# A hand-written order of pieces for VectorE, ScalarE and GpSimd in the attention part, from its ninth f-tile step

## The chip, the cores and the metric

The kernel runs on one core of one Trainium2 chip. The metric is the device time of one execution in microseconds (us); lower is better. The engines are TensorE (PE; its weight loads stand apart as PEld), VectorE (DVE), ScalarE (ACT), GpSimd (POOL) and SyncE (SP), which issues all of this kernel's data transfers (DMAs).

## The reference

Windowed attention with global tokens, a SiLU-gated two-matrix layer, and a second layer with a rational activation, on 4 batches of 544 rows (2176 rows of 512 values) in float32:

```python
def _attn_ref(q_l, k_l, v_l, q_g, k_g, v_g):
    ...
    s_g = scale * np.matmul(q_g, k_all.transpose(0, 1, 3, 2))
    out_g = np.matmul(sm(s_g), v_all)
    ...
    mask = np.abs(pos[:, None] - pos[None, :]) <= window
    s_ll = np.where(mask, s_ll, -1000000000.0)
    a_l = sm(np.concatenate([s_lg, s_ll], axis=-1))
    out_l = np.matmul(a_l, np.concatenate([v_g, v_l], axis=2))
    return np.concatenate([out_g, out_l], axis=2)

def _moe_ref(x, w_gate, w_val, w_out):
    g = x @ w_gate
    silu = g * (1.0 / (1.0 + np.exp(-g)))
    return (silu * (x @ w_val)) @ w_out

def _moe2_ref(x, w_in, w_out, a, b):
    h = x @ w_in
    P = a[0] + a[1] * h + a[2] * h * h + a[3] * h ** 3
    Q = 1.0 + np.abs(b[0]) * np.abs(h) + np.abs(b[1]) * h * h
    return (P / (Q + 1e-06)) @ w_out
```

The weights of the two layers arrive as float64. They are handed over as 64-bit words and made into float32 on the chip.

## The kernel before, in words

Three stages overlap: attention, the gated layer and the rational layer. A float32 product is made of three products of rounded halves (`mm3`, lines 526 to 528), so every operand of a layer is split into a high and a low half: ScalarE casts (L123, L374), VectorE subtracts (L126, L641).

Attention is cut into 24 units: a local unit is 128 rows of one batch, a global unit the 32 global rows of one batch, half of the heads. A unit passes through scores (`a_score`), the largest score (`a_least`, VectorE, L306 or L312 to L314), the exponentials (`a_exp`, ScalarE, L325 or L331 and L333), transposes (`a_turn`, L354), sums (`a_sums`, VectorE), copies to SBUF (`a_copy`, ScalarE), values (`a_value`), division (`a_norm`, VectorE, L427 or L433), a transpose back (`a_back`, L448) and a store into the rows x32 (`a_store`, VectorE, L374 or L461).

The gated layer's first four f-tiles of 128 (part "a") run while attention still goes on: 32 steps n = (row chunk c, f-tile). Steps 0 to 7, with the first nine units, are an order of words written by hand (`opening`). Steps 8 to 31 are a loop, four to a chunk of 256 rows (c = 2 and 4) or 288 rows (c = 3, 5, 6, 7). In a step TensorE makes the gate (12 matmuls), the transposes of unit t-1, the value product (12), the scores of unit t, the outward product of the step before (12, into four PSUM banks with the tag "a"), the values of unit t-1 and the transposes back of unit t-2. Steps 12, 20 and 27 to 31 have no attention. All other PSUM tiles have the tag "b" and share four banks in turn, so each waits for the readers of the tile four before it: the scores wait for the readers of the gate, the gate for those of the scores before, and so on.

Beside this the loop brings in the raw weights of the other f-tiles, 24 pieces: a DMA from HBM into a stage tile (`fetch`), a scaling on GpSimd (L141), a rounding on ScalarE (L143), two joins on VectorE (L144 and L146), and a DMA to the scratch w1s. When a chunk's four f-tiles are summed, `evac_a` copies the four banks (ScalarE L806, VectorE L804) into y tiles (four of them), and a DMA stores each to the scratch yas. In chunk 7 the weights come back from w1s and are split (ScalarE two casts, VectorE one subtraction, GpSimd one).

In the loop before, TensorE's and SP's order is the program's own. The order of VectorE, ScalarE and GpSimd is that of a planner, which has costs of its own for each operation and may move it ahead of others. From the gated layer's second part on (f-tiles 4 to 11, part "b") the order of all engines is the program's, in both kernels.

Of the kernel before, what the change touches and what calls it, by code (L numbers as in the profile page):

```python
# [21 lines left out]
S = SL + SG  # L22
# [55 lines left out]
def tile_attn_moe_moe(  # L78
# [48 lines left out]

    def fetch(src, pool, bufs):
# [7 lines left out]
    def to_f32(fetched):  # L136
        st, wide = fetched
        if wide:
            v = st.rearrange("p (c t) -> p c t", t=2)
            low, high = v[:, :, 0], v[:, :, 1]  # L140
            nc.gpsimd.tensor_scalar(out=high.bitcast(F32), in0=high.bitcast(F32), scalar1=2.0 ** -112,  # L141
                                    scalar2=1.0, op0=ALU.mult, op1=ALU.mult)
            nc.scalar.activation(low, low.bitcast(U32), AF.Copy, bias=0.25, scale=0.905 * 2.0 ** -29)  # L143
# [3 lines left out]
                                           op0=ALU.bitwise_and, op1=ALU.bitwise_or)  # L147
        return st[:, 0:512].bitcast(F32)
# [187 lines left out]
    def a_soft(u):  # L336
        for p in units[u][2] if units[u][1] < 4 else (0,):
            a_least(u, p)
            a_exp(u, p)

# [42 lines left out]

    def a_trans(u):
        ps_ = units[u][2] if units[u][1] < 4 else (0,)
        for p in ps_:
            a_turn(u, p)
        a_sums(u)
        for p in ps_:
            a_copy(u, p, nc.scalar)  # L390
# [45 lines left out]
    def a_pv(u):  # L436
        for p in units[u][2] if units[u][1] < 4 else (0,):
            a_value(u, p)
        a_norm(u)
        if u in local and local.index(u) + 2 < len(local):  # L440
            load_v(local[local.index(u) + 2])

# [21 lines left out]
    def a_out(u):  # L464
        a_back(u)
        a_store(u, nc.vector)

# [13 lines left out]
    def a_scores(u):  # L481
        a_loads(u)
        a_score(u)
        a_score2(u)
        a_soft(u)

    begun = set()

    def chunk_split(c, ks=range(4)):
        for k in ks:  # L490
            split_xy(("a", c), chunks_a[c], k)
# [4 lines left out]
    def attend(n, part):  # L496
        if n in step_at:
            t = step_at[n]
            for fn, u in (((a_trans, t - 1),), ((a_scores, t),), ((a_pv, t - 1), (a_out, t - 2)))[part]:
                if U0 <= u < NU or u == U0 - 1 and fn is not a_scores:  # L500
                    begun.add((fn, u))
                    fn(u)
# [46 lines left out]
    def hidden(key, f, w, inject):  # L549
        g = mlp(key, 0, f, w)  # L550
        s = p1.tile([128, N1P], F32, tag="s", name="s")
        h = p1.tile([128, 2, N1P], F32R, tag="h", name="h")
        if inject:
            nc.scalar.activation(s[:, :w], g[:, :w], AF.Tanh, scale=0.5)
            nc.vector.scalar_tensor_tensor(out=s[:, :w], in0=s[:, :w], scalar=1.0, in1=g[:, :w],
                                           op0=ALU.add, op1=ALU.mult)
            inject()
        else:
            nc.scalar.activation(s[:, :w], g[:, :w], AF.Silu)
        v = mlp(key, 1, f, w)  # L560
        if inject:
            nc.vector.scalar_tensor_tensor(out=s[:, :w], in0=s[:, :w], scalar=0.5, in1=v[:, :w],
                                           op0=ALU.mult, op1=ALU.mult)
        else:
            nc.vector.tensor_tensor(out=s[:, :w], in0=s[:, :w], in1=v[:, :w], op=ALU.mult)  # L565
        split(h[:, 0, :w], h[:, 1, :w], s[:, :w], nc.scalar, nc.vector)
        hs[key, f] = h
        if inject:
            inject()
# [92 lines left out]
    def w_scale(i):  # L662
        high = raw[i].rearrange("p (c t) -> p c t", t=2)[:, :, 1]
        nc.gpsimd.tensor_scalar(out=high.bitcast(F32), in0=high.bitcast(F32), scalar1=2.0 ** -112,
                                scalar2=1.0, op0=ALU.mult, op1=ALU.mult)

    def w_round(i, eng):
        lo = raw[i].rearrange("p (c t) -> p c t", t=2)[:, :, 0]
        nc.scalar.activation(lo, lo.bitcast(U32), AF.Copy, bias=0.25, scale=0.905 * 2.0 ** -29)

    def w_join(i):
        v = raw[i].rearrange("p (c t) -> p c t", t=2)
        lo, high = v[:, :, 0], v[:, :, 1]
        nc.vector.scalar_tensor_tensor(out=lo, in0=high, scalar=3, in1=lo,
                                       op0=ALU.logical_shift_left, op1=ALU.bitwise_or)
        nc.vector.scalar_tensor_tensor(out=raw[i][:, 0:512], in0=high, scalar=-2 ** 31, in1=lo,
                                       op0=ALU.bitwise_and, op1=ALU.bitwise_or)

# [8 lines left out]
    def act(word):  # L687
# [3 lines left out]
        u, p = (n + [0, 0])[:2]  # L691
# [35 lines left out]
        elif name in "FADHL":  # L727
            i = int(a)
            {"F": lambda: w_scale(i), "A": lambda: w_round(i, s), "D": lambda: w_join(i),
# [43 lines left out]
    state = {"n": 0}  # L773

    late = []

    def inject_a():
        g, i = state["g"], state["i"]
        c = seq_a[g][0]
        state["i"] = i + 1  # L780
        if c < NCA - 1:
            if i == 0 or i == 1 and g % 5 == 0:
                bg.end()
                bg.begin()
            else:
# [12 lines left out]

    def evac_a(c, j):
        for o, cols in [(0, chunks_a[0]), (HALF, chunks_a[1])] if c == 1 else [(0, chunks_a[c])]:  # L800
# [6 lines left out]
            for d, cc in xcols(cols):  # L807
                nc.sync.dma_start(yas[:, j, cc], y[:, d])
# [42 lines left out]
    for g, (c, f) in list(enumerate(seq_a))[2 * NA:]:  # L851
        if g == 8:
            loads["cb"]()
            loads["ca"]()
        if g == 16:
# [3 lines left out]
        state.update({"g": g, "i": 0})  # L859
        if (c, f) == (NCA - 1, 0):  # L860
            assert len(begun) == 4 * (NU - U0) + 3
# [5 lines left out]
            while bg.busy():  # L867
                bg.begin()
                bg.end()
            rest.prefetch(4)  # L870
        hidden(("a", c), f, w, inject_a)
# [286 lines left out]
```

## Time and profile before

| what | value |
|---|---|
| median of three runs | 938.31 us (934.78, 939.10, 938.31) |
| the profiled execution | 935.89 us |
| its span, first to last instruction | 934.1 us |
| TensorE busy in the span | 908.7 us (97%) |
| VectorE, ScalarE, GpSimd busy | 664.0, 569.4, 116.9 us |
| steps 8 to 31, by the start of their matmuls | 87.65 to 264.26 us of the span |

The profiled execution's own time is 1.8 us more than its span and lies between the three runs. Matmuls are pipelined, and the end of one is modelled: a matmul of 256 columns is shown with 0.28 us though the next starts 0.12 us after it.

### The profile page before, as it was taken

The page shows a single profiled execution, that of the slowest core. Times are in us where ns is not written, and L with a number is a line of the kernel's source. Part 1 is how long each engine was busy: PE and PEld are TensorE (multiplying, and loading weights), DVE is VectorE, ACT ScalarE, POOL GpSimd, SP SyncE. Part 2 cuts the span into 40 slices and gives each one's busy share as a digit, 9 for nine tenths or more (in the row PEclk, how much of TensorE's full clock was granted, in tenths as well). Part 3 has the DMA queues.
Part 4 walks back from the last instruction along what each step waited for, and adds up shares of the span by engine and source line. Part 5 has one row for each costly group of instructions (what it writes and reads, how often), then busy time and mean ns, then how long its engine had stood idle before and what let it go on. Part 6 is the DMA issues. An engine that isn't in the chain of part 4 may idle for free.

```text
span 934.1 us, 20234 instructions
## 1 busy us (share of the span) xinstructions
PE 908.7 (97%) x7893; PEld 845.8 (91%) x7895; DVE 664.0 (71%) x1578; ACT 569.4 (61%) x1348; POOL 116.9 (13%) x133
## 2 busy tenths in 40 slices
PE   6999999999999999999999999999999999999997
PEld 4789889788999999999999999999999999999896
DVE  4885778667735466555532569988889888888886
ACT  6764756555434344333322368888778788788796
POOL 1342010010303233111100001000000000000032
PEclk9999999999999999999999999999999999999999
DMA  9944996862551234454512230000010010010010
GB/s 330 370 148 156 318 345 219 285 233 83 167 197 46 89 98 140 147 183 153 177 57 72 77 105 1 1 22 13 1 35 0 1 35 1 1 35 1 1 35 24
DMA packets 51935, 102.76 MB, mean 110 GB/s; under 512 B 6912, under 2 KB 27008, under 8 KB 51840
## 3 DMA queue, kind: packets, MB, share of 16 engines
q1 hardware_dynamic: 51840, 101.47, 32.5%
q8 instruction: 62, 1.02, 0.4%
q14 instruction: 33, 0.27, 0.1%
HBM read 81.01 MB, written 20.45 MB: 109 GB/s over the span
## 4 chain that ended last, share of the span: by engine, by line
PE 84%; DMA 6%; DVE 4%; ACT 2%; issue 2%; SPq 1%; POOL 0%; POOLq 0%; ACTq 0%; DVEq 0%
PE b L526 15%; PE b L528 15%; PE b L527 15%; PE a L1056 7%; PE a L1055 6%; PE a L1054 6%; PE a L526 5%; PE a L527 4%; PE a L528 4%; DMA stage<-in_w_dram 4%; PE b L259 1%; PE b L354 1%; PE b L404 1%; DMA q<-in_qT_dram 1%; PE a L354 1%
## 5 line engine op out<-in xcount | busy, mean ns | idle before, releaser
L526 PE MATMUL b<-xy,wb 128*128 128x312 f32 (+3 forms) x632 | 197.5, 313 | 0.0
L528 PE MATMUL b<-xy,wb 128*128 128x312 f32 (+3 forms) x632 | 197.4, 312 | 0.0
L527 PE MATMUL b<-xy,wb 128*128 128x312 f32 (+3 forms) x632 | 197.4, 312 | 0.0
L526 PE MATMUL b<-xy,wa 128*128 128x256 f32 (+2 forms) x400 | 125.2, 313 | 5.8 <-DVE s L633 2.5
L527 PEld LDWEIGHTS b<-xy,wb 128*128 128x128 f32 x632 | 118.9, 188 | 2.5
L526 PEld LDWEIGHTS b<-xy,wb 128*128 128x128 f32 x632 | 118.9, 188 | 2.5
L527 PE MATMUL b<-xy,wa 128*128 128x256 f32 (+2 forms) x400 | 121.0, 302 | 0.0
L528 PE MATMUL b<-xy,wa 128*128 128x256 f32 (+2 forms) x400 | 120.9, 302 | 0.0
L528 PEld LDWEIGHTS b<-xy,wb 128*128 128x128 f32 x632 | 118.8, 188 | 0.0
L123 ACT CAST h<-s 128x312 fp32r<-128x312 f32 (+3 forms) x80 | 35.5, 444 | 118.2 <-DVE s L565 91.7
L565 DVE TENSOR_TENSOR s<-s,b 128x312 f32<-128x312 f32 (+1 forms) x56 | 26.7, 476 | 95.5 <-PE b L528 90.7
L1004 ACT ACTIVATE t<-b,cst 128x384 f32<-128x384 f32 (+1 forms) x94 | 61.3, 652 | 53.8 <-PE b L528 51.0
L526 PEld LDWEIGHTS b<-xy,wa 128*128 128x128 f32 x400 | 76.1, 190 | 9.3 <-DVE s L633 3.0
L1018 DVE TENSOR_TENSOR t<-t,b 128x384 f32<-128x384 f32 (+1 forms) x94 | 49.9, 531 | 41.5 <-ACT a L1005 41.3
L527 PEld LDWEIGHTS b<-xy,wa 128*128 128x128 f32 x400 | 75.8, 190 | 1.3
L528 PEld LDWEIGHTS b<-xy,wa 128*128 128x128 f32 x400 | 75.7, 189 | 0.0
L141 POOL TENSOR_SCALAR stage<-stage 128x512 f32<-128x512 f32 x56 | 39.2, 700 | 226.0 <-DMA stage<-in_w_dram 174.9
L1056 PE MATMUL a<-wb,g 128*128 128x512 f32 x170 | 67.1, 395 | 0.3 <-POOL g L1028 0.3
L1006 ACT ACTIVATE q<-a,cst 128x384 f32<-128x384 f32 (+1 forms) x94 | 64.9, 691 | 3.0
L1054 PE MATMUL a<-wb,g 128*128 128x512 f32 x170 | 66.3, 390 | 0.5 <-ACT g L1041 0.5
L1055 PE MATMUL a<-wb,g 128*128 128x512 f32 x170 | 66.7, 392 | 0.0
L126 DVE TENSOR_TENSOR h<-s,h 128x312 fp32r<-128x312 f32 (+3 forms) x80 | 39.4, 493 | 35.0 <-ACT h L123 34.8
(180 smaller groups left out, 2238.1 us busy)
## 6 DMA issues: line engine op xcount, KB each, us to landing
stage<-in_w_dram SPq DMA_DIRECT2D x68, 512.0 KB, 4.3
v<-in_vw_dram SPq DMA_DIRECT2D x16, 512.0 KB, 6.6
v<-in_vw_dram SPq DMA_DIRECT2D x16, 384.0 KB, 5.1
w1s<-stage SPq DMA_DIRECT2D x24, 256.0 KB, 5.3
stage<-w1s SPq DMA_DIRECT2D x12, 512.0 KB, 5.5
w2s<-stage SPq DMA_DIRECT2D x20, 256.0 KB, 2.4
stage<-w2s SPq DMA_DIRECT2D x10, 512.0 KB, 4.0
out_dram<-x SPq DMA_DIRECT2D x17, 256.0 KB, 2.8
```

The costliest lines, as they stand in the source:

```text
L123: nc.scalar.copy(hi, src)
L126: eng_lo.tensor_tensor(out=lo, in0=src, in1=hi.bitcast(F32), op=ALU.subtract)
L141: nc.gpsimd.tensor_scalar(out=high.bitcast(F32), in0=high.bitcast(F32), scalar1=2.0 ** -112, scalar2=1.0, op0=ALU.mult, op1=ALU.mult)
L526: nc.tensor.matmul(o, w[:, 0, wsl], x[:, 0, xsl], start=first, stop=False)
L527: nc.tensor.matmul(o, w[:, 0, wsl], x[:, 1, xsl], start=False, stop=False)
L528: nc.tensor.matmul(o, w[:, 1, wsl], x[:, 0, xsl], start=False, stop=last)
L1004: nc.scalar.activation(pt[n], h, AF.Identity, bias=NA2, scale=NA3)
L1006: nc.scalar.activation(pq[n], a, AF.Identity, bias=B0, scale=B1)
L1018: nc.vector.tensor_tensor(out=t, in0=t, in1=h, op=ALU.mult)
L1054: nc.tensor.matmul(o, g[:, 0, gsl], w[:, 0], start=(f == 0), stop=False)
L1055: nc.tensor.matmul(o, g[:, 0, gsl], w[:, 1], start=False, stop=False)
L1056: nc.tensor.matmul(o, g[:, 1, gsl], w[:, 0], start=False, stop=(f == F2 - 1))
```

## The change

Two things change in steps 8 to 31. First, VectorE, ScalarE and GpSimd follow a written list, as TensorE and SP do. A step is a line of words, one line for steps whose unit t is local, one for the rest, and one for chunk 7. A word is a piece: G gate, V value, O outward, t tanh, g and v the two multiplications, h and l the halves of the hidden tile, T R C P N S M E X Z the pieces of attention in the order of the list above (R sums, C copies, P values, N division, S scores, M largest, E exponentials, X back, Z store), F A D W the raw weight's scaling, rounding, joins and store, y and Y the halves of the next chunk's rows, e the copies of finished sums, w their stores, r a weight of chunk 7, q the loads of later units. The order of TensorE's own pieces is as before.

Second, work is moved between steps. A raw weight is scaled in one step, and rounded, joined and stored in the next; five steps (11, 16, 22, 24, 25) scale two, so that steps 12, 17, 23, 25 and 26 round and join two. The stores of finished sums are put off to a later word, mostly in the next step. The rows of chunks 4 and 5 are split in steps 14 and 15, and 18 and 19. The loads of queries, keys and values of later units are issued at a step's end, and look one unit further ahead.

The diff, cut to its core (helpers that only changed their name or were no longer called are left out):

```diff
...
-    def hidden(key, f, w, inject):
+    def hidden(key, f, w):
         g = mlp(key, 0, f, w)
         s = p1.tile([128, N1P], F32, tag="s", name="s")
         h = p1.tile([128, 2, N1P], F32R, tag="h", name="h")
-        if inject:
-            nc.scalar.activation(s[:, :w], g[:, :w], AF.Tanh, scale=0.5)
-            nc.vector.scalar_tensor_tensor(out=s[:, :w], in0=s[:, :w], scalar=1.0, in1=g[:, :w],
-                                           op0=ALU.add, op1=ALU.mult)
-            inject()
-        else:
-            nc.scalar.activation(s[:, :w], g[:, :w], AF.Silu)
+        nc.scalar.activation(s[:, :w], g[:, :w], AF.Silu)
...
-    def inject_a():
-        g, i = state["g"], state["i"]
-        c = seq_a[g][0]
-        state["i"] = i + 1
-        if c < NCA - 1:
-            if i == 0 or i == 1 and g % 5 == 0:
-                bg.end()
-                bg.begin()
-            else:
-                bg.end()
-        if c < NCA - 1:
-            attend(g, i)
-            if seq_a[g + 1][0] > c and i:
-                chunk_split(c + 1, (2 * i - 2, 2 * i - 1))
-        for _ in range(2):
-            if late and late[0][0] < state["n"]:
-                late.pop(0)[1]()
-        state["n"] += 1
-        if c == NCA - 1 and (3 * g + i) % 2:
-            rest.begin()
-            rest.end()
+    stores = []
+    def put_stores():
+        while stores:
+            stores.pop(0)()
...
-                nc.sync.dma_start(yas[:, j, cc], y[:, d])
+                stores.append(lambda d=d, cc=cc, y=y: nc.sync.dma_start(yas[:, j, cc], y[:, d]))
...
-    def bg_back(i, item, st):
-        nc.sync.dma_start(w1s[i // 2, :, 512 * (i % 2):512 * (i % 2) + 512], st)
-
-    bg = Loader(rest_items, lambda i, x: fetch(w1[x[0], :, x[1]], *((pro, 4) if i % 6 < 4 else (const, 2))), bg_back, 3)
+    bg_raw = {}
+    bg = {"F": 0, "A": 0, "D": 0, "W": 0}
+    BG_TWO = (11, 16, 22, 24, 25)
+
+    def bg_fetch(upto):
+        while len(bg_raw) < min(upto, NR):
+            i = len(bg_raw)
+            f, m = rest_items[i]
+            bg_raw[i] = fetch(w1[f, :, m], *((pro, 4) if i % 6 < 4 else (const, 2)))[0]
+
+    def bg_step(name, n):
+        if name == "F":
+            count = 0 if n >= 27 else 1 + (n in BG_TWO)
+        else:
+            count = bg["F"] - bg[name] if name == "A" else bg["A" if name == "D" else "D"] - bg[name]
+        for _ in range(count):
+            i = bg[name]
+            bg[name] = i + 1
+            if name == "F":
+                bg_fetch(i + 1)
+                wide_scale(bg_raw[i])
+            elif name == "A":
+                wide_round(bg_raw[i])
+            elif name == "D":
+                wide_join(bg_raw[i])
+            else:
+                bg_fetch(i + 4)
+                nc.sync.dma_start(w1s[i // 2, :, 512 * (i % 2):512 * (i % 2) + 512],
+                                  bg_raw[i][:, 0:512].bitcast(F32))
...
-    def out_a():
-        pc, pf, pw = prev
-        outward(("a", pc), pf, pw, pf == 0, pf == NA - 1)
-        if pf == NA - 1 and pc:
-            late.extend((state["n"], lambda c=pc, j=j: evac_a(c, j)) for j in range(KD))
+    SPLITS = {11: (3, (0, 1, 2, 3)), 14: (4, (0, 1)), 15: (4, (2, 3)), 18: (5, (0, 1)), 19: (5, (2, 3)),
+              23: (6, (0, 1, 2, 3)), 27: (7, (0, 1, 2, 3))}
+    STEP = {
+        "local": "G A F T0 T1 R D t C0 C1 g e W w y V Y v h S M0 E0 l M1 E1 O e P0 P1 X Z q N",
+        "global": "G A F t T0 T1 R C0 C1 e D g W w y Y V S v e M0 h O P0 P1 E0 X Z q N l",
+        "last": "G r w t g V O v B h r e r l",
+    }
+    now, pend, evacs = {}, {"t": [], "g": [], "v": [], "h": [], "l": []}, []
...
+        if name == "G":
+            s = p1.tile([128, N1P], F32, tag="s", name="s")
+            pend["t"].append((s[:, :w], mlp(("a", c), 0, f, w)[:, :w], c, f, w))
+        elif name == "V":
+            now["val"] = mlp(("a", c), 1, f, w)[:, :w]
+        elif name == "t":
+            s, g, *rest_ = pend["t"].pop(0)
+            nc.scalar.activation(s, g, AF.Tanh, scale=0.5)
+            pend["g"].append((s, g, *rest_))
+        elif name == "g":
+            s, g, *rest_ = pend["g"].pop(0)
+            nc.vector.scalar_tensor_tensor(out=s, in0=s, scalar=1.0, in1=g, op0=ALU.add, op1=ALU.mult)
+            pend["v"].append((s, *rest_))
+        elif name == "v":
+            s, *rest_ = pend["v"].pop(0)
+            nc.vector.scalar_tensor_tensor(out=s, in0=s, scalar=0.5, in1=now["val"], op0=ALU.mult, op1=ALU.mult)
+            pend["h"].append((s, *rest_))
+        elif name == "h" and pend["h"]:
+            s, c, f, w = pend["h"].pop(0)
+            h = p1.tile([128, 2, N1P], F32R, tag="h", name="h")
+            nc.scalar.copy(h[:, 0, :w], s)
+            pend["l"].append((s, h, c, f, w))
+        elif name == "l" and pend["l"]:
+            s, h, c, f, w = pend["l"].pop(0)
+            low(nc.vector, h[:, 0, :w], h[:, 1, :w], s)
+            hs[("a", c), f] = h
+        elif name == "O":
+            pc, pf, pw = now["prev"]
+            outward(("a", pc), pf, pw, pf == 0, pf == NA - 1)
+            if pf == NA - 1:
+                evacs.extend((pc, j) for j in (1, 0, 3, 2))
+        elif name == "e":
+            if evacs and c == 2:
+                put_stores()
+            for pc, j in evacs[:2 if c == 2 else 4]:
+                evac_a(pc, j)
+            del evacs[:2 if c == 2 else 4]
+        elif name == "w":
+            put_stores()
+        elif name in "yY":
+            if n in SPLITS:
+                c, ks = SPLITS[n]
+                for k in ks:
+                    if name == "y":
+                        xs[("a", c), k] = xy_tile(c)
+                    t = xs[("a", c), k]
+                    for d, cc in xcols(chunks_a[c]):
+                        if name == "y":
+                            nc.scalar.copy(t[:, 0, d], x32[:, k, cc])
+                        else:
+                            low(nc.vector, t[:, 0, d], t[:, 1, d], x32[:, k, cc])
+        elif name == "B":
+            split_xy(("b", 0), chunks_b[0], f)
+        elif name == "r":
+            now["r"] += 1
+            if (3 * n + now["r"]) % 2:
+                rest.begin()
+                rest.end()
+        elif name in "FADW":
+            bg_step(name, n)
+        elif name == "q":
+            if t is not None:
+                a_loads(t + 1)
+                if t - 1 in local and local.index(t - 1) + 2 < len(local):
+                    load_v(local[local.index(t - 1) + 2])
+        elif t is not None and name in "TRCPNSMEXZ":
+            u = t - 1 if name in "TRCPN" else t if name in "SME" else t - 2
+            if U0 - 1 <= u < NU and (p == 0 or units[u][1] < 4):
+                act(name + "%d" % p, u)
...
+    bg_fetch(3)
+    ordered = [tc.manual_schedule()]
+    ordered[0].__enter__()
+    for n, (c, f) in list(enumerate(seq_a))[2 * NA:]:
...
+        now.update(n=n, c=c, f=f, w=w, t=step_at.get(n), prev=prev, r=-1)
...
-        hidden(("a", c), f, w, inject_a)
-        out_a()
-        inject_a()
+        for word in STEP["last" if c == NCA - 1 else "local" if now["t"] in local else "global"].split():
+            step(word)
         prev = (c, f, w)
-        if c == NCA - 1:
-            split_xy(("b", 0), chunks_b[0], f)
+    while pend["h"] or pend["l"]:
+        step("h")
+        step("l")
...
```

## Rows read from the trace of the kernel before

**Rows 1.** Windows: TensorE, weight loads, VectorE, ScalarE, GpSimd busy; clock; DMA.

```profile
87.65:264.26 176.61, 169.62 (x2576) 153.71 (x2574) 127.09 (x419) 102.91 (x341) 24.98 (x30) 0.99 0.70 235
...
152.05:168.29 16.24, 16.24 (x353) 14.96 (x354) 11.26 (x56) 12.10 (x52) 0.70 (x1) 1.00 0.88 282
...
264.26:934.10 669.84, 664.79 (x3998) 629.67 (x3996) 474.79 (x939) 413.21 (x829) 65.17 (x69) 1.00 0.18 57
```

**Rows 2.** Waits of TensorE in steps 8 to 31: total us, times, longest.

```profile
PE b L526 <- DVE mn L306: 2.1, 1, 2.1
PE b L526 <- ACT e L331: 0.9, 1, 0.9
PE b L271 <- DVE s L555: 0.9, 1, 0.9
PE a L526 <- ACT h L123: 0.9, 1, 0.9
PE b L354 <- ACT xy L123: 0.7, 1, 0.7
PE b L358 <- DVE x L427: 0.5, 1, 0.5
PE b L526 <- DVE x L374: 0.3, 1, 0.3
PE a L526 <- DVE y L804: 0.3, 1, 0.3
```

**Rows 3.** Window right behind the longest wait, columns as in rows 1.

```profile
202.00:205.40 3.40, 3.40 (x17) 3.38 (x16) 1.70 (x9) 2.82 (x11) 0.00 (x0) 0.50 0.90 247
```

**Rows 4.** Timeline of GpSimd and VectorE around 198 us: start, us, instruction.

```profile
198.29 0.64 POOL L141 TENSOR_SCALAR stage<-stage 128x512 f32<-128x512 f32 x1 [6.87 <-DMA stage<-in_w_dram]
...
198.99 0.69 DVE L144 SCALAR_TENSOR_TENSOR stage<-stage 128x512 int32<-128x512 int32 x1 [2.87 <-POOL stage L141]
```

**Rows 5.** Waits of all engines, 87 to 269 us.

```profile
ACT stage L143 <- DMA stage<-in_w_dram: 15.1, 12, 2.6
...
DVE stage L144 <- POOL stage L141: 11.0, 9, 2.9
```

**Rows 6.** Timeline of VectorE in an undisturbed stretch, steps 16 and 17.

```profile
159.42 0.69 DVE L144 SCALAR_TENSOR_TENSOR stage<-stage 128x512 int32<-128x512 int32 x1 [0.46 <-POOL stage L141]
...
160.76 0.68 DVE L427 TENSOR_TENSOR x<-b,rc 128x512 f32<-128x512 f32 x1
...
168.01 0.69 DVE L427 TENSOR_TENSOR x<-b,rc 128x512 f32<-128x512 f32 x1 [0.75 <-PE b L404]
168.62 0.68 DVE L374 COPY x<-b 128x512 f32<-128x512 f32 x1
169.22 0.16 DVE L366 TENSOR_SCALAR sm<-sm 128x8 f32<-128x8 f32 x1
```

**Rows 7.** Timeline of TensorE, step 17 (256 rows): gate, scores, transposes back.

```profile
160.17 0.36 PE L526 MATMUL b<-xy,wa 128*128 128x256 f32 x1
...
164.15 1.16 PE L259 MATMUL b<-k,q 64*32 64x128 f32 x64
...
167.88 0.66 PE L448 MATMUL b<-ident,x 128*128 128x128 f32 x4
```

**Rows 8.** Timeline of TensorE, gate and scores of step 15 (288 rows).

```profile
143.80 0.38 PE L526 MATMUL b<-xy,wa 128*128 128x288 f32 x1
...
148.05 0.41 PE L259 MATMUL b<-k,q 64*32 64x128 f32 x11
```

**Rows 9.** DMA issues, steps 8 to 31: count, KB each, median us to landing.

```profile
v<-in_vw_dram SPq DMA_DIRECT2D x8, 512.0 KB, 6.2
yas<-y SPq DMA_DIRECT2D x28, 128.0 KB, 3.2
```

**Rows 10.** Timeline of GpSimd and VectorE at 147 us.

```profile
147.31 0.66 POOL L141 TENSOR_SCALAR stage<-stage 128x512 f32<-128x512 f32 x1 [2.64 <-DMA stage<-in_w_dram]
...
147.35 1.23 DVE L146 SCALAR_TENSOR_TENSOR stage<-stage 128x512 int32<-128x512 int32 x1
```

More of the change, by code (lines that the diff above doesn't have):

```diff
@@ L134, in fetch, with wide_scale, wide_round, wide_join @@
         return st, src.dtype == I64
-    def to_f32(fetched):
-        st, wide = fetched
-        if wide:
+    def wide_scale(st):
+        if RAW64:
+            high = st.rearrange("p (c t) -> p c t", t=2)[:, :, 1]
+            nc.gpsimd.tensor_scalar(out=high.bitcast(F32), in0=high.bitcast(F32), scalar1=2.0 ** -112,
+                                    scalar2=1.0, op0=ALU.mult, op1=ALU.mult)
+    def wide_round(st):
+        if RAW64:
+            low = st.rearrange("p (c t) -> p c t", t=2)[:, :, 0]
+            nc.scalar.activation(low, low.bitcast(U32), AF.Copy, bias=0.25, scale=0.905 * 2.0 ** -29)
+    def wide_join(st):
+        if RAW64:
             v = st.rearrange("p (c t) -> p c t", t=2)
             low, high = v[:, :, 0], v[:, :, 1]
-            nc.gpsimd.tensor_scalar(out=high.bitcast(F32), in0=high.bitcast(F32), scalar1=2.0 ** -112,
-                                    scalar2=1.0, op0=ALU.mult, op1=ALU.mult)
-            nc.scalar.activation(low, low.bitcast(U32), AF.Copy, bias=0.25, scale=0.905 * 2.0 ** -29)
             nc.vector.scalar_tensor_tensor(out=low, in0=high, scalar=3, in1=low,
@@ L147, in to_f32 @@
                                            op0=ALU.bitwise_and, op1=ALU.bitwise_or)
+    def to_f32(fetched):
+        st, wide = fetched
+        assert wide == RAW64
+        wide_scale(st)
+        wide_round(st)
+        wide_join(st)
         return st[:, 0:512].bitcast(F32)
@@ L434, in a_norm @@
                                         op0=ALU.mult)
[L436 to L441, printed above, removed]
     def a_back(u):
@@ L479, in tile_attn_moe_moe @@
     U0 = 9
[L481 to L491, printed above, removed]
     step_at = dict(zip([n for n in range(8, 27) if n not in (12, 20)], range(U0, NU + 2)))
     assert step_at[26] == NU + 1
[L496 to L502, printed above, removed]
     xs, hs, accs = {}, {}, {}
@@ L685, in w_low, with act @@
         low(eng, w[:, 0], w[:, 1], raw.pop(i)[:, 0:512].bitcast(F32))
-    def act(word):
+    def act(word, unit=None):
         other = word[-1] == "*"
@@ L690, in act @@
         n = [int(x) for x in a if x.isdigit()]
-        u, p = (n + [0, 0])[:2]
+        u, p = (n + [0, 0])[:2] if unit is None else (unit, n[0])
         s, v, g = nc.scalar, nc.vector, nc.gpsimd
@@ L728, in act @@
             i = int(a)
-            {"F": lambda: w_scale(i), "A": lambda: w_round(i, s), "D": lambda: w_join(i),
+            {"F": lambda: wide_scale(raw[i]), "A": lambda: wide_round(raw[i]), "D": lambda: wide_join(raw[i]),
              "H": lambda: w_high(i, s), "L": lambda: w_low(i, v if other else g)}[name]()
@@ new lines, in tile_attn_moe_moe, with step @@
+    STEP = {
[3 rows of a table added]
+    }
+    now, pend, evacs = {}, {"t": [], "g": [], "v": [], "h": [], "l": []}, []
+    def step(word):
+        n, c, f, w, t = (now[x] for x in "ncfwt")
+        name, p = word[0], int(word[1:] or 0)
+        if name == "G":
[67 more added lines that the diff above has]
+                act(name + "%d" % p, u)
@@ L858, in tile_attn_moe_moe @@
         w = wide(chunks_a[c])
-        state.update({"g": g, "i": 0})
+        now.update(n=n, c=c, f=f, w=w, t=step_at.get(n), prev=prev, r=-1)
         if (c, f) == (NCA - 1, 0):
-            assert len(begun) == 4 * (NU - U0) + 3
+            assert not st_z and not st_x and bg["W"] == NR
             pro_cm.__exit__(None, None, None)
@@ L933, in tile_attn_moe_moe @@
         w = wide(chunks_b[c])
-        hidden(("b", c), f, w, None)
+        hidden(("b", c), f, w)
         if 0 < c < NCB - 1:
```

50 lines of the change are left out of this document (5 added, 45 removed).

## The prediction

> **What bounds the kernel now.** I read the windows first. Behind the changed stage TensorE is busy 664.79 of 669.84 us, so the rest of the kernel is TensorE's, and time saved in steps 8 to 31 comes through whole. Steps 8 to 31 take 176.61 us, of which TensorE is busy 169.62: 6.99 us are idle. VectorE is busy 127.09 and ScalarE 102.91, so neither is the bound as a sum; only their order can cost TensorE anything [rows 1]. Two neighbouring steps, 16 and 17, show the stage without loss: 16.24 us, all of it busy, 8.12 us a step [rows 1].
>
> Then TensorE's waits, which say who ended each idle time. The reader is to see that the 6.99 us are a few single waits, not something that every step pays: 2.1 on the largest scores (L306), 0.9 on a global unit's exponentials, 0.9 on the gate's multiplication (L555), 0.5 and 0.3 on a division and a store, 0.9 on a hidden tile in chunk 7, 0.7 on ScalarE behind row splits, 0.3 on a finished sum's copy [rows 2].
>
> Third, the timeline at the longest one. VectorE sat idle for 2.87 us in front of a join (L144) that waited for GpSimd's scaling, which had itself waited for the raw weight to land; the scores' largest values stood behind that join [rows 4]. This is one case of a class: VectorE waited nine times, 11.0 us in all, for a scaling [rows 5]. By the order on VectorE's timeline, the waits on L306, L331, L555, L427 and L374 all have such a join ahead of what TensorE wanted (for L331 ahead of the largest score that its exponential needs): 2.1 + 0.9 + 0.9 + 0.5 + 0.3 = 4.7 us [rows 2].
>
> Last, the clock. After the 2.1 us wait the granted clock is 0.50 for the 3.40 us from 202.00 on, the 1.2 GHz level, with TensorE busy throughout [rows 3]. Half of that work would have fitted: 1.7 us more.
>
> **What can be removed.** Idle 7.0 and clock 1.7 make 8.7 us. The idle time is counted from a modelled end: a 256-wide matmul is shown with 0.28 us and the next starts 0.12 behind it, so each wait hides some 0.16 more. Ten waits, the eight shown and a few short ones, make 1.6 (an estimate). So 10.3 us is the ceiling; TensorE's own order and its matmuls don't change.
>
> **The edits one by one.**
>
> *Raw weights a step apart.* No instruction is added: 24 scalings, roundings, join pairs and stores remain. A piece is fetched three steps before it is scaled, some 24 us, where the slowest kind of input takes 6.2 [rows 9], and its join comes a step after the scaling. So no join should stand waiting for GpSimd, and the 4.7 us, their 5 x 0.16 hidden, and the clock's 1.7 go: 7.2.
>
> *The list in chunk 7 and in step 11.* The wait on the hidden tile (0.9) came when the planner ran four split weights together; the list places one or two in each of four steps. The 0.7 on row splits came from splits set ahead of the tanh; the list has them behind the copies. With their hidden parts 1.9. What is left of the ceiling, 1.2, is short waits that I also take as gone, and charge anew where the list makes them.
>
> *What the list costs.* I lay one local step of 256 rows from its gate's start. The scores begin at 164.15 - 160.17 = 3.98 [rows 7], and by the turn of the four banks they wait until the gate's multiplication has read the gate. On VectorE that multiplication stands behind Z, N, R and the joins. Z waits for the transposes back, which end at 168.54, 0.25 after the next gate's start (168.29, the window's end) [rows 1, 7]. A pass over 512 values holds the engine 168.62 - 168.01 = 0.61, and the first R comes 0.60 after the store [rows 6]. So Z at 0.25, N at 0.86, R at 1.46, the joins near 1.8 (R's two small operations, an estimate from 0.16 each and the hand-over). A join pair holds 160.76 - 159.42 = 1.34 [rows 6], the multiplication about 0.4 (an estimate from 0.68 for 512 values): done at 3.5. Slack 0.45, and in 288-row steps, where scores begin at 148.05 - 143.80 = 4.25 [rows 8], 0.7. An ordinary step costs nothing; its cover is this slack.
>
> Where a step has two join pairs the sum grows by 1.34. Step 17: done at 4.87, 0.9 late. Step 23 (288 rows, and Z is a short one): 0.45. Step 13 follows step 12, which is short, has no attention, and carries two pairs: 0.4. Step 19 has the last hidden half ahead of R and only five transposes on TensorE: 0.3. Step 25 has two pairs and copies of sums, but no scores: 0.1.
>
> Step 9 has a different wait. The four y tiles filled at the end of step 8 must be stored before the other two banks are copied, and on SP these stores stand behind two value loads that wait for step 8's values. Stores land 3.2 us after issue alone, 6.2 if they drag behind the loads [rows 9]. The outward product wants the third bank some 5.8 us into step 9 (3.98 + 1.1 + 0.8). With issue 1 to 2 us into the step, the copies come 0 to 2 us late; I take 1.0. Together 0.9 + 0.45 + 0.4 + 0.3 + 0.1 + 1.0 = 3.15 us, bounds 0 and 6.
>
> SP's own order: the loads of the last global units wait at the end of step 19 for values of step 21, and weights 16 and 17 are behind them. They would be issued at the end of step 21, land about 6 us later, and are rounded in step 23: a margin of some 3 us, so nothing.
>
> *GpSimd and VectorE.* A scaling that began at 147.31 and took 0.66 lies over a join of 1.23 that began at 147.35, against 0.69 elsewhere: 0.54 more [rows 10, 4]. I allow one such hit on a step without slack, 0.5, bounds 0 and 8.6 (16 x 0.54).
>
> The Trainium skill, "SBUF — State Buffer", section "Who interferes with whom", says that a VectorE instruction with two SBUF inputs and a GpSimd instruction that reads SBUF take turns at a shared port, the later one blocked until the first is done. The trace agrees: 147.97 + 0.69 is 148.66, and the join ended at 148.58. By that rule the list would pay whenever a scaling meets the joins of a step, and the sum could be up to 8.6 worse, as in the first rival.
>
> **Sum.** 10.3 - 3.15 - 0.5 = 6.6 us less. The profiled execution took 935.9 (span 934.1 and 1.8 around it), so 929.3 by its account. The three runs' median, 938.3, is 2.4 above it, with runs on both sides; I go half way: **930.5**.
>
> **Rivals.**
>
> *The port eats it.* Scalings meet the joins or multiplications in most attention steps: 16 x 0.54 = 8.6 at most, half of it likely in this case: 930.5 + 4.3 = 934.8, and 939 with all. For it: nothing ties the scaling to a place. Against it: fetches go out early in a step and land near 6 us later, when VectorE is at the scores, and one join in 24 was stretched before.
>
> *Step 9 becomes the long wait.* The stores drag 6.2 us or more, TensorE stands 3.5 us instead of 1.0, and the clock falls as it did behind the 2.1 us wait, 1.7 more: about 934.7.
>
> *Slower: ScalarE's rounding at the head of the step.* It comes first in ScalarE's list, in front of tanh and copies. If raw weights land late it blocks all of these. Before, 12 roundings waited 15.1 us, 1.26 each [rows 5]. If all 24 wait so, less 0.45 of slack, 24 x 0.81 = 19 us are added: 930.5 + 19 = 950. It decides from some 9 late pieces on. Against it: three steps between fetch and use.
>
> *It doesn't do what it says.* The order differs in places that TensorE doesn't feel, and the waits move: 936 to 938.
>
> **Chances and range.** Forecast 0.65, port 0.12, step 9 0.10, late rounding 0.09, no effect 0.04. About 0.5% (4.7 us) is what a measurement of this kernel can tell from no change. The forecast alone counts as faster; port, step 9 and no effect lie within 0.5%; late rounding is slower: 0.65, 0.26, 0.09. Low end: the whole ceiling and no new waits, 935.9 - 10.3 = 925.6, taken as 926. High end: the cases within 0.5% but for their last half microsecond, 937.5; the late rounding is left out.
>
> **What would show it.** Right: no VectorE wait on a scaling; TensorE's waits on L306, L331 and L427 gone; clock 1.00 from 90 to 260; steps 8 to 31 near 170 us; waits of 0.5 to 1 in steps 9 and 17 on a copy and on the gate's multiplication. Wrong: a wait of 2 us or more with a clock of 0.50 behind it, roundings waiting for landings, stretched joins in many steps, or a wait at every step on the exponentials or on the gate's multiplication, which would mean that my one-step layout misplaces a piece.

## The result, and the profile after

The changed kernel takes **928.9 us** (median of 4 runs, 927.6 to 930.1), the kernel before 938.3 beside it: ratio 0.991, 95% interval 0.988 to 0.994. Forecast were 930.5, within 926 to 937.5, and faster. The profiled execution took 928.4 us with a span of 926.3; the sum in the prediction gave 929.3 for it.

The windows of the changed kernel (columns as in [rows 1]), steps 8 to 31 and all that follows:

```profile
85.47:253.23 167.76, 165.18 (x2576) 151.76 (x2574) 128.25 (x419) 101.52 (x340) 23.46 (x28) 1.00 0.72 237
253.23:926.28 673.05, 667.98 (x3998) 632.36 (x3996) 477.80 (x942) 414.72 (x832) 65.76 (x70) 1.00 0.18 59
```

Against [rows 1], steps 8 to 31 are 8.85 us shorter: 4.41 are idle time of TensorE (6.99 to 2.58), 4.44 are busy time with the same matmuls (169.62 to 165.18). Of the latter 1.70 is the half-clock stretch that is gone (clock 1.00), the other 2.74 are what is left, put down to the time that a wait hides under the modelled end of a matmul (no row shows it by itself). The opening ended 2.18 us sooner; its list is the same, and in the 13 executions here that share it, it ended between 85.3 and 88.9 us, so that is an execution's own. The rest took 3.2 us *longer*, which nobody had forecast (last section). What follows goes by steps 8 to 31; three executions with the changed kernel's order took 167.76, 166.91 and 166.63.

TensorE's waits in those steps, the whole answer (line, releaser: total us, times, longest):

```profile
PE b L365 <- ACT s L810: 1.4, 2, 0.7
PE a L498 <- DVE y L726: 0.8, 1, 0.8
PE a L498 <- ACT y L728: 0.2, 1, 0.2
```

All eight rows of [rows 2] are gone but for the wait for a copied sum, which was forecast for step 9, and the 0.7 us at a transpose of step 11, which stands here under another name (last section). The row that matters most is missing. Here are ScalarE's roundings (L147, before L143):

```profile
L147 ACT ACTIVATE stage<-stage x24: 647/668/698, 94.4 to 230.1; 128x512 int32<-128x512 uint32 x24
...
its engine sat idle before it (us, times) until:
who waited for it (us, times):
  DVE stage L153: 0.8, 1
```

Between "until:" and "who waited" stands nothing: no rounding waited for a landing, where 12 waited 15.1 us before [rows 5]. VectorE's 11.0 us of waiting for scalings are gone too. The prediction took VectorE's wait for the loss; whether that is all of it, the experiments ask.

### The profile page after: what moved, and what is told of

It reads as the page before. It is cut to its first block, busy times and chain, and to the rows that moved or that the text cites. A ratio compares the mean times of both kernels' runs of the same rounds, so it can differ in the third digit from the quotient of the medians.

```text
span 926.3 us, 20214 instructions
## 1 busy us (share of the span) xinstructions
PE 907.4 (98%) x7895; PEld 845.5 (91%) x7895; DVE 667.2 (72%) x1578; ACT 569.3 (61%) x1348; POOL 116.4 (13%) x133
## 3 DMA queue, kind: packets, MB, share of 16 engines
q8 instruction: 62, 1.02, 0.4%
## 4 chain that ended last, share of the span: by engine, by line
PE 94%; DVE 2%; ACT 1%; DMA 1%; issue 1%; SPq 0%; POOL 0%; POOLq 0%; ACTq 0%
PE b L498 17%; PE b L499 17%; PE b L500 17%; PE a L1077 7%; PE a L1078 7%; PE a L1076 6%; PE a L498 5%; PE a L499 5%; PE a L500 5%; PE b L275 2%; PE b L365 1%; PE b L407 1%; PE b L444 1%; PE b L418 1%; DMA q<-in_qT_dram 1%
## 5 line engine op out<-in xcount | busy, mean ns | idle before, releaser
L123 ACT CAST h<-s 128x312 fp32r<-128x312 f32 (+1 forms) x56 | 25.3, 453 | 91.7 <-DVE s L527 91.7
L141 POOL TENSOR_SCALAR stage<-stage 128x512 f32<-128x512 f32 x68 | 47.7, 705 | 234.7 <-DMA stage<-in_w_dram 174.5
L525 ACT ACTIVATE s<-b 128x312 f32<-128x312 f32 (+1 forms) x56 | 24.0, 428 | 66.6 <-PE b L500 66.6
```

Of the source, the lines that this page charges most:

```text
L123: nc.scalar.copy(hi, src)
```

## Experiments

**What carries the gain.** Three kernels give parts of steps 8 to 31 back to the planner. The moved pieces stay in the emission; only `manual_schedule` changes. Here and below, a kernel without a ratio was executed once.

```
# e2_planner: none          e3_vector_alone: PE, SP, DVE      e4_scalar_alone: PE, SP, Activation
-    ordered = [tc.manual_schedule()]
+    ordered = [tc.manual_schedule(engines={...})]
```

> The moved pieces are emitted as in the changed kernel, a step apart, but all engines of steps 8 to 31 are ordered by the planner again, as before. Theory (the step apart is most of the gain, 7.2 of 10.3 us in the prediction's sum): no join waits for a scaling, steps 8 to 31 take 168 to 171 us, the whole 929 to 932. Rival (the written order is what gains): the planner again sets joins or splits ahead of the largest scores, waits of 0.5 to 2 us on VectorE return, 174 to 177 us, the whole 935 to 938.

> In steps 8 to 31 only TensorE, SyncE and VectorE follow the written list; ScalarE and GpSimd are ordered by the planner. Theory (a join that stands in VectorE's order before its raw weight has landed was the loss, so VectorE's order alone carries the gain): steps 8 to 31 take 168 to 170 us, no join waits for a scaling over 1 us. Rival (ScalarE's order carries as much: with the planner's roundings between tanh and copies the waits on the transposes' copies and exponentials return): 171 to 175 us.

> The other half: TensorE, SyncE and ScalarE follow the written list, VectorE and GpSimd are ordered by the planner. Theory (VectorE's order carries the gain): waits on the largest scores or the gate's multiplication behind joins that wait for scalings stay, steps 8 to 31 take 172 to 176 us. Rival (ScalarE's order carries it): 168 to 170 us.

Times: 935.99 us with the planner alone (ratio 1.000, 0.998 to 1.003), 942.4 with VectorE's list alone, 927.5 with ScalarE's. So my theory fell three times. Waits of ScalarE and VectorE with the planner alone, whose steps 8 to 31 take 174.96 us:

```profile
ACT stage L147 <- DMA stage<-in_w_dram: 11.1, 9, 2.8
...
DVE stage L153 <- POOL stage L141: 10.8, 8, 2.9
```

Emitting the pieces a step apart gives nothing by itself: the waits are nearly those of before, 11.0 and 15.1 [rows 5]. With VectorE's list alone, first the windows:

```profile
86.78:267.37 180.59, 170.54 (x2575) 155.79 (x2574) 129.00 (x421) 102.80 (x343) 24.40 (x29) 0.97 0.66 222
```

Then its waits, of ScalarE and TensorE:

```profile
ACT stage L147 <- DMA stage<-in_w_dram: 23.4, 17, 5.8
...
PE b L287 <- ACT et L385: 3.0, 2, 2.8
...
PE b L498 <- ACT e L347: 2.1, 3, 1.7
PE b L275 <- ACT et L385: 2.1, 1, 2.1
```

No join waits for a scaling any more, and the stage is *longer* than before. Seventeen roundings wait for landings, and what stands behind them on ScalarE holds TensorE: scores (L275, L287) wait for the copies of the transposes (L385), the gate for the exponentials (L347), 3.0 + 2.1 + 2.1 = 7.2 us in all. The loss has not gone, it has moved from VectorE to ScalarE. With ScalarE's list alone (windows):

```profile
85.35:252.54 167.19, 165.10 (x2575) 151.68 (x2574) 127.25 (x419) 101.59 (x342) 23.95 (x28) 1.00 0.72 238
```

Neither a rounding waits for a landing nor a join for a scaling in this kernel, though VectorE is ordered by the planner. A join needs its rounding as well as its scaling. So where ScalarE's list puts the rounding behind the landing, a join can at most wait for that rounding: nine did, 2.6 us in all, the longest 0.8 (waits of VectorE). How the planner places the joins then is not shown; that ScalarE's list alone gives the gain is.

**One piece moved.** Two kernels keep the whole list and move the rounding a step forward, into the step of its scaling: one with join and store, one alone.

```
# e5_same_step: F ahead of A in both lists; join and store follow in the same step
-        "local": "G A F T0 ...            +        "local": "G F A T0 ...
# e11_round_early: that, and the join stays a step behind
+            if name == "A":
+                bg["rounded"] = bg["A"]
-            ... bg["A" if name == "D" else "D"] - bg[name]
+            ... bg["rounded" if name == "D" else "D"] - bg[name]
```

> The written list stays, but scaling, rounding, join and store of a raw weight fall in the same step (scaling ahead of rounding in the list), so rounding and join come one step, some 8 us, earlier. Theory (the step apart matters): in the changed kernel weights 16 and 17 were scaled only 3.3 and 2.7 us ahead of their joins, so in step 22 the rounding at the head of ScalarE's list waits some 5 us for a landing, and tanh and copies behind it; TensorE stands 2 to 5 us, the clock falls behind it, steps 8 to 31 take 171 to 177 us. Rival (GpSimd scales whatever has landed long before, the list alone does it): 167.5 to 168.5 us, no wait over 0.5 us that the changed kernel has not.

> The changed kernel with one thing moved: ScalarE's rounding of a raw weight stands one step earlier, in the step of its scaling; join and store stay where they were. Theory (a rounding that stands in ScalarE's order ahead of the landing is the loss, since tanh, copies and exponentials queue behind it): in step 22 the rounding waits 4 to 5.5 us for weights 16 and 17, TensorE stands 3 to 4 us as in the run with everything in one step, steps 8 to 31 take 171.5 to 174 us. Rival (the join on VectorE that waits for GpSimd is the loss, as the prediction had it): the joins still come after the scalings, so 167 to 168.5 us.

Steps 8 to 31 took 173.36 us with everything in one step (934.9 in all), 174.64 with the rounding alone (938.4). With the rounding alone no join waits for a scaling, and yet its timeline of ScalarE and TensorE in step 22 reads:

```profile
195.58 0.18 ACT L341 ACTIVATION_READ_ACCUMULATOR e<-e,mn 128x1 f32 x1
201.03 0.65 ACT L147 ACTIVATE stage<-stage 128x512 int32<-128x512 uint32 x1 [5.26 <-DMA stage<-in_w_dram]
203.19 0.65 ACT L147 ACTIVATE stage<-stage 128x512 int32<-128x512 uint32 x1 [1.51 <-DMA stage<-in_w_dram]
203.75 0.39 ACT L812 ACTIVATE s<-b 128x288 f32<-128x288 f32 x1
204.04 1.06 ACT L385 COPY et<-b 128x512 f32<-128x512 f32 x2
...
204.67 0.69 PE L275 MATMUL b<-k,q 64*32 64x128 f32 x16 [5.51 <-ACT et L385]
```

And its window right behind:

```profile
206.50:210.00 3.50, 3.50 (x32) 3.15 (x28) 2.15 (x17) 2.94 (x15) 1.33 (x2) 0.50 0.26 104
```

The whole chain stands there: a rounding at the head of ScalarE's step waits 5.26 us for its weight, tanh and copies queue behind it, the scores wait 5.51 us for the copy, and the clock is 0.50 behind that. It fits the theory; TensorE stood longer than the 3 to 4 us expected, so the stage is 0.6 above that range. A late rounding thus costs by itself: no join waits for GpSimd here. That a waiting join costs nothing does not follow. The table below counts five roundings that waited for weights; a sixth waited 2.5 us, which the profile puts down to a store.

**Fetching sooner instead.** In the kernel before, one number:

```
-    bg = Loader(..., bg_back, 3)
+    bg = Loader(..., bg_back, 5)
```

> The kernel before with one number changed: raw weights are fetched two pieces sooner (five ahead, not three); everything is ordered by the planner as before. Theory (late landings under the planner's early roundings are most of the 8.85 us): ScalarE's wait for landings falls from 15.1 us to under 6, steps 8 to 31 take 170 to 173 us, the whole 931 to 934. Rival (the planner's order loses by itself, wherever the weights are): 175 to 177 us, the whole 936 to 939.

This took 939.8 us, ratio 1.003 (1.001 to 1.006), steps 8 to 31 176.29: the rival's time, and nothing was gained. But the roundings' wait only fell from 15.1 us to 9.2 in 8 places (two more, 1.2 us, are put down to stores), not below 6, and joins still waited 8.9 us in 8. So two pieces more of lead do not replace the order; what weights that land in time would do under the planner was not reached.

**Step 9 and the held stores.**

```
-                stores.append(lambda ...: nc.sync.dma_start(yas[:, j, cc], y[:, d]))
+                nc.sync.dma_start(yas[:, j, cc], y[:, d])
```

> The stores of the finished sums are issued where their copies stand in the list, not held back for later. Theory (the step apart of the sum stores costs in step 9): in step 8 the four stores go ahead of the value loads on SyncE, land some 1 us earlier, and the waits of 0.95 and 0.31 us in step 9 fall to 0.3 together; steps 8 to 31 take 166.7 to 167.2 us. Rival (held stores keep SyncE free for the weights): a store that waits for its copy holds up the fetches and the weights' stores behind it, raw weights land later, and roundings or joins wait: 168 to 171 us.

Steps 8 to 31 took 166.16 us (929.5 in all), below the 166.7 expected, and TensorE's waits for a copied sum in step 9 are gone: holding the stores back costs the 1.0 us of waits there. The rival's price showed too, at one place (ScalarE's and VectorE's waits):

```profile
ACT stage L147 <- DMA stage<-in_w_dram: 2.9, 2, 2.5
DVE stage L153 <- POOL stage L141: 2.2, 2, 1.5
```

The 2.5 us are the second rounding of step 23, weight 17; behind it TensorE waited 0.6 us for a copy and 1.0 for an exponential.

**VectorE's slack.** Behind the joins of each attention step (17 in all, 34 passes), two more passes over 512 values on a tile that nothing reads:

```
+            if name == "D" and t is not None:
+                for _ in range(2):
+                    nc.vector.scalar_tensor_tensor(out=more, in0=more, scalar=3, in1=more, ...)
```

> Every attention step gets two more VectorE passes over 512 values right behind the joins, on a tile of its own that nothing reads: 1.4 us more, as much as one more join pair. The prediction's layout (slack 0.45 to 0.7 us before the scores wait for the gate's multiplication) gives 0.7 to 0.95 us in each of 16 steps, 11 to 15 us: 179 to 183 us. The reading of the trace after (the scores did not wait for it, they began 0.7 us before it in step 17; TensorE next needs VectorE at the division and the next transposes) gives waits only in the steps with two pairs, 0 to 4 us: 168 to 172 us.

Steps 8 to 31 took 173.87 us, 6.1 to 7.2 more than the changed kernel: between the two. TensorE's first two waits and the one at the scores (933.4 in all):

```profile
PE b L498 <- ACT e L347: 2.8, 3, 1.1
PE b L498 <- DVE s L814: 0.5, 1, 0.5
...
PE b L275 <- ACT et L385: 0.3, 1, 0.3
```

The slack is used up, but not where the prediction placed it: no row has the scores waiting for the gate's multiplication. The largest waits come behind the global units' exponentials (L347), which follow VectorE's largest score.

**The gate ahead of the copies.** In the local list `g` was put ahead of `C0 C1`:

> Only the place of the gate's multiplication in the written list of the local steps changes (ahead of ScalarE's two copies); the order of the instructions on every engine stays, only the turn of the PSUM banks becomes the one that the prediction assumed. Theory (the bank turn is why the charged waits did not come): the scores now wait for the gate's multiplication where a step has two join pairs, about 0.9 us in step 17 and 0.3 to 0.45 in steps 13, 19 and 23, so steps 8 to 31 take 169 to 170 us instead of 167.8. Rival (the prediction laid VectorE's step too tightly and the turn does not matter): no wait on the gate's multiplication, 167.5 to 168.1 us.

The edit did nothing: the two words belong to different engines, so the order on each engine stayed the same, and in both traces the scores wait for the same engine's semaphore: ScalarE's in seven of the nine local steps, VectorE's in two. The run is a second execution of it in all but the names of buffers: 166.91 us, 927.0 in all. What sets the turn of the banks was not tested. A third, of the changed kernel unaltered (166.63 us; 927.2 in all, ratio to before 0.992, 0.990 to 0.995):

> The changed kernel once more, unaltered, to see what of a trace belongs to the kernel and what to a single execution. If the 2.8 us that its 384-column matmuls of the last layer took longer (156.06 us for 959 spacings, against 153.27 before) are the kernel's own, they are 155.9 to 156.2 us again; if they are a matter of the execution, 153.3 to 154.5 us can come. The waits of 0.9 us in steps 11 and 23, if they are bound to the place in TensorE's stream, lie at the same transposes again or are absent, at no other; steps 8 to 31 take 166.5 to 168 us; the opening, the same in all these kernels, ends between 85.3 and 88.6 us.

**A version meant to beat both.** First sums stored at once, weights fetched one piece sooner; then the same with TensorE's stream shifted.

```
# b1_stores_and_lead (in evac_a; the held form stays for the other chunks)
+                if c == 1:
+                    nc.sync.dma_start(yas[:, j, cc], y[:, d])
-                bg_fetch(i + 4)        +                bg_fetch(i + 5)        # and bg_fetch(3) -> (4)
# b2_shift: that, and
-            nc.tensor.matmul(idle, zero[:, 0:128], zero, ...)             # 11 times
+            nc.tensor.matmul(idle[:, 0:64], zero[:, 0:128], zero[:, 0:64], ...)   # 88 times
```

> A version meant to beat both: the first two chunks' sums are stored at once (the others a step later, as in the changed kernel) and raw weights are fetched one piece sooner. Theory (step 9's 1.26 us is the held stores; the late weights 16 and 17 of step 23 come from their place behind the last global units' loads on SyncE): no wait in step 9 over 0.4 us, none in step 23 on a copy or an exponential, steps 8 to 31 take 165.5 to 166.5 us, the whole 926 to 928.5. Rival (the sooner fetches push value loads back, and these are late instead): 167 to 170 us, the whole 928 to 932.

> The version with the two repairs (first sums stored at once, weights one piece sooner), and the 11 opening matmuls on zeros of 512 columns replaced by 88 of 64 columns, so that every later instruction of TensorE stands 154 places further on in its stream. Theory (the wait at the third transpose of step 23, 0.9 to 1.3 us, is a block of TensorE's instructions arriving late, bound to the place in the stream): it leaves that transpose, and any such wait lies 154 places, some 3 to 4 us of work, earlier; steps 8 to 31 take 164 to 165.5 us. Rival (it is ScalarE's tanh or copies in step 23): the wait of 0.9 to 1.3 us stays at the third transpose, 165.4 us as without the shift. The whole 925 to 928.

The first gives 165.44 us for steps 8 to 31, the shortest but one, and 927.6 in all (ratio 0.991, 0.988 to 0.993): in the trace 1.2 to 2.3 us better than the changed kernel, in the whole not to be told from it. Of TensorE's waits one is left, at the second transpose of step 23, where the changed kernel has it at the third (waits, the whole answer; L813 is the tanh):

```profile
PE b L365 <- ACT s L813: 1.2, 1, 1.2
```

With the shift it is no longer there (the last row is at another transpose, in step 18):

```profile
PE b L498 <- ACT e L347: 0.7, 1, 0.7
PE b L365 <- issue: 0.2, 1, 0.2
```

So it looks like a wait of TensorE's stream, not of ScalarE's tanh, which the view names; one execution alone would not show it, the last section does. No new one came 154 places earlier, as the theory had it. The 0.7 stands where other kernels showed 0.2 to 1.1. The opening ended at 89.92 us, so the whole, 930.2 (0.993, 0.990 to 0.995), missed the 925 to 928 expected and gained nothing.

All of it side by side; waits are those of the roundings for landings in steps 8 to 31:

| kernel | order of ScalarE | waits us, times | steps 8 to 31 |
|---|---|---|---|
| before | planner | 15.1, 12 | 176.61 |
| before, sooner fetch | planner | 9.2, 8 | 176.29 |
| pieces apart, planner | planner | 11.1, 9 | 174.96 |
| VectorE's list alone | planner | 23.4, 17 | 180.59 |
| rounding a step sooner | list | 8.2, 5 | 174.64 |
| all in one step | list | 5.3, 1 | 173.36 |
| stores at once | list | 2.9, 2 | 166.16 |
| ScalarE's list alone | list | none | 167.19 |
| changed kernel, three executions | list | none | 167.76, 166.91, 166.63 |
| first sums at once, sooner fetch | list | none | 165.44 |
| the same, TensorE's stream shifted | list | none | 165.20 |
| added VectorE work | list | none | 173.87 |

More waiting does not cost in proportion (it depends on what stands behind), but without waits no kernel here is above 168 except the one with added VectorE work.

## Why the prediction was right, and which steps were not

**The bound, and time saved in the stage comes through whole:** right in kind; the rest then moved by its own 3.2 us, a term the sum did not have.

**Raw weights a step apart, 7.2 us:** the waits went as said, but not by the step apart alone, which left most of them in place under the planner (174.96 us), and the prediction looked at one engine of two. Its reading of the longest wait holds: there VectorE's join, begun at 198.99 [rows 4], stood in front of the largest scores. ScalarE's rounding had waited for the same landing, but was done at 198.90, and ScalarE then waited 1.03 us more for the largest score (timeline of the kernel before):

```profile
198.23 0.67 ACT L143 ACTIVATE stage<-stage 128x512 int32<-128x512 uint32 x1 [2.60 <-DMA stage<-in_w_dram]
199.93 0.40 ACT L325 ACTIVATE e<-e,mn 128x128 f32<-128x128 f32 x1 [1.03 <-DVE mn L306]
```

What the prediction left out is the rounding: with the joins free of waits and the roundings not, the stage took 174.64 and 180.59 us. So either engine's wait for the late weight can hold TensorE. The written order of ScalarE alone took both away (167.19 us); the step apart is needed as the place of the rounding in that order.

**Hidden time, 1.6 us:** mis-sized, if the 2.74 by which busy time fell beside the clock's 1.70 are hidden time.

**The list in chunk 7 and in step 11, 1.9 us:** chunk 7's wait is gone. Step 11 still had 0.72 us at the third transpose in the first execution, and none in the second and third, with its splits behind the copies in all three. So the 0.7 of before, at the same place, was no wait for the row splits, as the prediction had it: like that of step 23 it was a wait for TensorE's instructions (last section).

**What the list costs, 3.15 us:** the failed term. Step 9 was forecast with 1.0 and showed 0.8 + 0.2. The other 2.15, in steps 13, 17, 19, 23 and 25, did not come. VectorE ran step 17 as laid out, within 0.13 us (the gate starts at 156.16; timeline of the changed kernel):

```profile
158.02 0.69 DVE L153 SCALAR_TENSOR_TENSOR stage<-stage 128x512 int32<-128x512 int32 x1
...
158.49 1.07 ACT L385 COPY et<-b 128x512 f32<-128x512 f32 x2
...
160.04 1.16 PE L275 MATMUL b<-k,q 64*32 64x128 f32 x64
160.08 0.75 DVE L155 SCALAR_TENSOR_TENSOR stage<-stage 128x512 int32<-128x512 int32 x1
160.73 0.43 DVE L814 SCALAR_TENSOR_TENSOR s<-s,b 128x256 f32<-128x256 f32 x1
```

The scores began 0.69 us *ahead* of the multiplication that I had them wait for. The sentence that failed is "by the turn of the four banks they wait until the gate's multiplication has read the gate". Here they wait for ScalarE's copies of the transposes (L385, done at 159.56, so no wait in this step), as the kernels with waits on L385 show. By its semaphore the wait was for ScalarE in the kernel before too, for the very scores of [rows 7]. I had worked the releaser out from the four banks and not read it.

**SP's own order, a margin of some 3 us in step 23, so nothing:** no wait came, but the margin was thinner. GpSimd's scalings show when weights 16 and 17 had landed, ScalarE's line when they were rounded (timeline of the changed kernel):

```profile
198.76 0.67 POOL L141 TENSOR_SCALAR stage<-stage 128x512 f32<-128x512 f32 x1 [16.19 <-DMA stage<-in_w_dram]
200.70 0.66 POOL L141 TENSOR_SCALAR stage<-stage 128x512 f32<-128x512 f32 x1 [1.28 <-DMA stage<-in_w_dram]
...
200.97 1.22 ACT L147 ACTIVATE stage<-stage 128x512 int32<-128x512 uint32 x2
```

The first has 2.2 us, the second (0.6 into the pair) some 0.9. Storing the sums at once was enough to lose it. Nor was 6.2 us the slowest kind of input: two loads of keys (672 KB) took 7.5 in the kernel before.

**GpSimd and VectorE, 0.5 us:** two second passes of a join took 1.02 and 1.01 us under a scaling instead of 0.69, and TensorE did not wait for either: 0. The Trainium skill, "SBUF — State Buffer", section "Who interferes with whom", agrees with those two; nothing else in the stage turned on it.

**The sum:** 10.3 - 3.15 - 0.5 = 6.6 against 8.85. By its terms: 2.15 of waits that did not come, 0.5 for the port, 1.1 of hidden time, less 1.4 for two waits at transposes that were not forecast, make 2.35 of the 2.25 missing. The opening's 2.2 us less and the rest's 3.2 us more leave 1.0 more, which takes off nearly half of the 2.25. That the whole came within a microsecond of 929.3 is in part luck.

**The rivals:** port, step 9 as a long wait, and no effect did not happen. The slower one, roundings at the head of the step that wait for landings, I gave 0.09 and set apart from the gain. It starts from the same late landing as the loss of the kernel before, with ScalarE held in place of VectorE, and one step's move of the rounding brings it on.

## What to carry to other kernels

When two engines wait at the same late transfer, ask which of them has TensorE's next need queued behind it: take the wait away on one engine at a time, and look whether the loss goes or moves to the other. A piece that waits for a transfer belongs in its engine's order behind the landing, and writing down one engine's order may be enough. A wait on a buffer is read from who released that matmul in the trace, not worked out from a ring of buffers.

## Unexpected on the chip

**TensorE waits for its own instructions.** Of the 11 executions whose TensorE follows the list, eight have a wait at one of the first three transposes of step 23 (five at the third), 0.3 to 1.2 us by the profile; the two with a moved rounding have none, nor has the one whose stream was shifted by 154 places. The profile's page has a queue for instructions (packets, MB, share):

```profile
q8 instruction: 62, 1.02, 0.4%
```

The traces show that it is TensorE's and that these waits are for it. Counted by their start, TensorE's matmuls, weight loads and own waits make 15884 instructions in the changed kernel, 256 to a packet. The waits of step 23, and all over 0.1 us that the profile puts down to nothing ("issue") but one at 13 us in five executions, stand 191 to 194 places behind a multiple of 256, in all 14 traces, the shifted one too. By this account the next block of instructions begins there. Over 0.1 us there are 52 waits at these places, and all but one (for VectorE, in the opening) end 1.2 to 1.5 us after a packet of queue 8 has landed, whoever the profile names; at no such place did TensorE go on sooner than 1.2 us behind the landing. In step 23 of the changed kernel the packet landed at 201.74 and TensorE went on at 203.12. With the stream shifted the block begins 154 places earlier in the work, where its packet had landed 5.2 us before. The longest such waits are in the opening (timelines of the changed kernel and of the shifted one):

```profile
22.82 0.42 PE L275 MATMUL b<-k,q 64*32 64x128 f32 x7 [3.29 <-issue]
25.33 0.55 PE L407 MATMUL a<-v,et 128*32 128x64 f32 x25 [2.67 <-issue]
```

The Trainium skill, "Runtime: NRT & Kernel Launch", section "Instruction fetch mechanics", says that instructions come in blocks of 256 and that crossing a block is mostly hidden. The traces agree: 51 of some 840 crossings show a wait over 0.1 us. What makes a packet late was not tested.

**The last layer's 384-column matmuls have two or three speeds.** The same 600 matmuls with the same tiles: in the changed kernel, and again in its repeat,

```profile
L498 PE MATMUL b<-xy,wb 128*128 128x384 f32 x200 | 67.6, 338 | 0.0
```

and with the added VectorE work, as before the change,

```profile
L498 PE MATMUL b<-xy,wb 128*128 128x384 f32 x200 | 67.1, 336 | 0.0
```

From start to start, the 883 of all 128x384 matmuls that another one follows sum to 156.06 us in the changed kernel and its repeat, 153.27 before, and to 154.4 in the kernel with the gate ahead of the copies, whose engines have the same order. The repeat gave the same sum, so it looks like a kernel's own; it costs 2.8 of the 3.2 us above, and what sets it stays open.
